# When GpSimd's indirect stores of rows may start: a table of waits in an attention and mixture-of-experts kernel

## The chip, the cores and the metric

The kernel runs on one core of a Trainium2 chip. The metric is the device time of one execution in microseconds (us). Three executions of the kernel before took 683.65 to 687.44 us, with a median of 686.25 us.

## What is computed

The reference runs a gated linear recurrence (an attention with a decaying state) and feeds its output to a mixture of experts. Cut to what matters:

```python
for t in range(S):                                   # attention, per batch and head
    S_re, S_im = (ar * S_re - ai * S_im + kv, ar * S_im + ai * S_re)   # kv = outer(k[t], v[t])
    y[:, :, t] = einsum('bhd,bhde->bhe', q[:, :, t], S_re)
x = y as [3072 tokens, 384]
noisy_logits = x @ w_gate + log1p(exp(x @ w_noise)) * noise            # 8 experts
top2 and their softmax weights
for e in range(8):                                   # each token goes to 2 of 8 experts
    out[mask] += top2_w * (relu(x[mask] @ w1[e]) @ w2[e])
```

## The kernel before, in words

The 3072 tokens are cut into 24 units of 128 tokens. Four units, one of each batch, make a group, so there are six groups; the code counts them 0 to 5, and the text calls them the first to the sixth group. An attention unit transposes its queries and keys on TensorE (`tr_unit`, L583) and copies them out on ScalarE (L584), forms scores (`sc_unit`, L593), masks them on VectorE (L594), and makes the output (`y_unit`, L642 and L644). `x_unit` (L652, L653) turns the output into rows of tokens in the tile `xr`.

When a group's rows are there, the gate picks two experts for each token (`gsel`, on ScalarE and VectorE), and `gdis` works out a slot for each choice: TensorE counts (L697, L699), and four VectorE instructions follow, L701 (positions), L703 (the running base), L704 and L707 (the slots, tile `sl`). Then `gscat` stores the rows: GpSimd issues one indirect store per unit and choice (L715), which sends 128 rows of 400 floats to the slots in the DRAM tensor `xs`. A group has eight such stores, and the kernel 48. The fifth and the sixth group are handled in two parts, of three units (`gscat4_0_3`, `gscat5_0_3`, six stores) and of one (`gscat4_3_4`, `gscat5_3_4`, two stores). The experts' phase loads rows from `xs` (L795, L797, L804). The first loads, of experts 0 and 1, wait only for the stores of the first three groups; the loads of the rest wait for all.

`xr` has three buffers. When a group opens a buffer again, GpSimd clears its last columns (MEMSET, L633) and copies the token numbers into it (L634). That MEMSET waits for the stores which read the buffer before, and it stands in GpSimd's queue between the stores.

Two tables set the order. `ORDER` lists, for TensorE (PE), ScalarE (ACT), VectorE (DVE) and SyncE (SP), every instruction of this phase in the sequence in which the engine runs them; `gdis3_0_4.0` is the first DVE instruction of `gdis` for group 3. GpSimd (POOL) has no list there. `PACE` adds waits: each entry makes one instruction wait for the end of a named instruction on another engine. Most entries concern the stores: `("POOL", "gscat3_0_4.2"): ("ACT", "gsel4_0_3.2")` lets the third store of group 3 start when that ScalarE instruction has ended. An engine works its queue in order, so what stands behind a waiting store on GpSimd waits too.

The loop that reads the table:

```python
for (e, t), (e2, t2) in PACE.items():
    tc.add_manual_dep(QUEUE[e, t][0], QUEUE[e2, t2][-1].name, later, reason="pace")
```

Of the kernel before, what the change touches and what calls it, by code (L numbers as in the profile page):

```python
# [187 lines left out]
        gsel3_0_4.6 gsel3_0_4.10 gsel3_0_4.7 gsel3_0_4.8 p319.0 st_upd16.0 gsel3_0_4.14 p3q19_0.0 sc_unit17_0.0  # L188
        sc_unit17_1.0 p322.0 st_scale15.0 gsel3_0_4.9 gsel3_0_4.12 gsel3_0_4.13 pick.4 gsel3_0_4.11 gsel3_0_4.16
        gsel3_0_4.17 p3q19_1.0 gsel3_0_4.15 gsel3_0_4.18 sc_unit18_0.0 gsel3_0_4.19 gsel3_0_4.22 gsel3_0_4.20  # L190
        st_upd17.0 sc_unit18_1.0 p321.0 p3q20_0.0 p3q21_0.0 p323.0 p3q20_1.0 gsel3_0_4.21 p3q22_0.0 st_upd18.0
        sc_unit19_0.0 sc_unit19_1.0 load_w10.0 gturn4_0_3.0 gsel4_0_3.0 p3q22_1.0 gdis3_0_4.0 gsel4_0_3.1 gsel4_0_3.2
        gdis3_0_4.1 x_G0_0.0 gsel4_0_3.3 load_w10.1 x_T0_0_0.0 gsel4_0_3.4 gsel4_0_3.5 gsel4_0_3.6 load_w10.2
        x_T0_0_1.0 gturn4_3_4.0 sc_unit20_0.0 gsel4_0_3.7 sc_unit20_1.0 gsel4_0_3.9 gsel4_3_4.0 x_T0_0_2.0 gsel4_0_3.8
        gsel4_3_4.1 gsel4_3_4.2 st_scale16.0 st_scale16.1 gdis3_0_4.2 gsel4_3_4.3 gsel4_0_3.11 gsel4_0_3.14 p3q21_1.0
        gsel4_0_3.15 x_G0_0.2 gsel4_0_3.12 p3q23_0.0 gsel4_0_3.10 mm10_0_1.0 gsel4_0_3.16 gsel4_0_3.17 gsel4_0_3.13
        gdis3_0_4.3 mm10_0_2.0 x_G0_0.1 mm10_0_1.1 gsel4_0_3.20 st_scale17.0 mm10_0_2.1 p3q23_1.0 gsel4_3_4.4
        st_upd19.1 st_upd23.0 gsel4_3_4.5 gsel4_3_4.6 st_upd15.0 sc_unit21_0.0 gsel4_0_3.18 sc_unit21_1.0 gsel4_3_4.7
        gdis4_0_3.0 gsel4_0_3.19 gdis4_0_3.1 load_w20_0_1_2.0 gsel4_3_4.10 gsel4_3_4.8 gsel4_3_4.9 st_scale19.0
        st_scale18.0 gsel4_3_4.16 gdis4_0_3.2 gdis4_0_3.3 load_w20_0_1_2.2 sc_unit22_0.0 gdis4_3_4.0 gdis4_3_4.1  # L200
# [72 lines left out]
}  # L273


# [1255 lines left out]
```

## Time and profile before

| | us |
|---|---|
| median of 3 executions | 686.25 |
| lowest and highest | 683.65, 687.44 |
| the profiled execution, its own time | 686.77 |
| span of its instructions in the trace | 685.1 |
| TensorE matmul busy in the span | 650.1 (95%) |
| VectorE busy | 435.1 (64%) |
| ScalarE busy | 367.9 (54%) |
| GpSimd busy | 174.9 (26%) |
| mean granted TensorE clock | 0.985 of full speed |

The busy shares are averages over unlike stages. Until about 268 us the kernel works on attention and gating, with expert 0's first matmuls between; from then on TensorE works through the experts. The chain that ended last is 77% TensorE and 11% VectorE.

### The profile page before, as it was taken

The page shows a single profiled execution, that of the slowest core. Times are in us where ns is not written, and L with a number is a line of the kernel's source. Part 1 is how long each engine was busy: PE and PEld are TensorE (multiplying, and loading weights), DVE is VectorE, ACT ScalarE, POOL GpSimd, SP SyncE. Part 2 cuts the span into 40 slices and gives each one's busy share as a digit, 9 for nine tenths or more (in the row PEclk, how much of TensorE's full clock was granted, in tenths as well). Part 3 has the DMA queues.
Part 4 walks back from the last instruction along what each step waited for, and adds up shares of the span by engine and source line. Part 5 has one row for each costly group of instructions (what it writes and reads, how often), then busy time and mean ns, then how long its engine had stood idle before and what let it go on. Part 6 is the DMA issues. An engine that isn't in the chain of part 4 may idle for free.

```text
span 685.1 us, 14285 instructions
## 1 busy us (share of the span) xinstructions
PE 650.1 (95%) x5505; PEld 573.5 (84%) x5505; DVE 435.1 (64%) x971; ACT 367.9 (54%) x610; POOL 174.9 (26%) x183
## 2 busy tenths in 40 slices
PE   8999999997989788999999999999999999999995
PEld 3468786876878577989899899899899899899895
DVE  7899999987778547546556526735735736746411
ACT  6999999987646345264423622732632732723300
POOL 3000000135230426002513302152142142163311
PEclk9999999999899889999999999999999999999998
DMA  6937766758386555278654756698598697682201
GB/s 240 295 113 205 212 158 211 199 177 258 118 249 182 184 165 171 87 252 236 173 159 118 264 143 203 198 192 223 189 166 250 193 186 228 194 219 91 83 36 35
DMA packets 120012, 124.24 MB, mean 181 GB/s; under 512 B 73610, under 2 KB 99104, under 8 KB 119936
## 3 DMA queue, kind: packets, MB, share of 16 engines
q1 hardware_dynamic: 110672, 95.76, 48.4%
q0 software_dynamic: 9264, 27.48, 13.3%
q8 instruction: 45, 0.74, 0.4%
q14 instruction: 31, 0.25, 0.1%
HBM read 70.11 MB, written 42.90 MB: 165 GB/s over the span
## 4 chain that ended last, share of the span: by engine, by line
PE 77%; DVE 11%; ACT 4%; another core or an unknown queue 2%; DMA 2%; issue 2%; SPq 1%; POOL 0%; POOLq 0%; ACTq 0%
PE ph L966 29%; PE po L1002 24%; PE po L1027 6%; PE ptr L583 3%; PE psc L593 2%; PE cum L533 2%; PE pY L642 2%; PE pY L644 1%; PE psc L966 1%; DVE qk L565 1%; DVE am L594 1%; DVE qh L573 1%; PE cum L652 1%; DVE im L528 1%
## 5 line engine op out<-in xcount | busy, mean ns | idle before, releaser
L966 PE MATMUL ph<-x,w1h 128*128 128x512 f32 (+4 forms) x720 | 184.7, 345 | 0.0
L1002 PE MATMUL po<-w2h,h 128*128 128x384 f32 x640 | 164.2, 335 | 0.0
L966 PEld LDWEIGHTS ph<-x,w1h 128*128 128x128 f32 x720 | 125.2, 188 | 14.9 <-DVE x L949 0.2
L987 POOL DMA_INDIRECT out_dram<-ao,ox x54 | 58.0, 1073 | 258.4 <-DVE ao L1015 155.4
L966 PE MATMUL ph<-x,w1l 128*128 128x512 f32 (+4 forms) x360 | 123.9, 344 | 0.0
L1002 PEld LDWEIGHTS po<-w2h,h 128*128 128x128 f32 x640 | 115.8, 188 | 0.3
L968 ACT ACTIVATE h<-ph 128x512 fp32r<-128x512 f32 (+4 forms) x120 | 60.7, 511 | 101.0 <-PE ph L966 82.2
L971 DVE SCALAR_TENSOR_TENSOR h<-ph,h 128x512 fp32r<-128x512 f32 (+5 forms) x128 | 69.3, 548 | 60.2 <-ACT h L968 55.3
L1002 PE MATMUL po<-w2l,h 128*128 128x384 f32 x320 | 107.0, 334 | 0.0
L715 POOL DMA_INDIRECT xs<-xr,sl x48 | 54.1, 1127 | 201.7 <-DVE kh L573 127.3
L1015 DVE SCALAR_TENSOR_TENSOR ao<-po,gw,ao 128x384 f32<-128x384 f32 (+1 forms) x42 | 25.7, 612 | 101.5 <-PE po L1002 101.3
L966 PEld LDWEIGHTS ph<-x,w1l 128*128 128x128 f32 x360 | 67.6, 188 | 7.6
L948 ACT CAST x<-xj 128x512 fp32r<-128x512 f32 (+4 forms) x39 | 20.7, 531 | 87.1 <-DVE xj L945 86.2
L978 POOL DMA_INDIRECT ao<-out_dram,ox x47 | 54.5, 1160 | 32.5 <-issue 28.8
L1002 PEld LDWEIGHTS po<-w2l,h 128*128 128x128 f32 x320 | 60.1, 188 | 0.2
L593 PEld LDWEIGHTS psc<-qT,kT 112*64 112x64 f32 x768 | 37.6, 143 | 5.9 <-issue 3.9
L593 PE MATMUL psc<-qT,kT 112*64 112x128 f32 (+1 forms) x768 | 41.1, 257 | 1.1 <-ACT kT L584 0.6
L644 PE MATMUL pY<-am,v 128*48 128x128 f32 x384 | 37.2, 277 | 5.0 <-issue 2.3
L594 DVE TENSOR_TENSOR am<-psc,mask 128x512 f32<-128x512 f32 x48 | 32.3, 680 | 13.6 <-PE psc L593 7.2
L1027 PE MATMUL po<-h,w2h 128*128 128x272 f32 (+2 forms) x192 | 38.7, 294 | 0.0
L949 DVE TENSOR_TENSOR x<-xj,x 128x512 fp32r<-128x512 f32 (+4 forms) x39 | 22.6, 579 | 24.1 <-ACT x L948 24.1
L584 ACT ACTIVATE kT<-ptr 112x1024 f32<-112x1024 f32 x24 | 24.8, 1032 | 22.7 <-remote 14.8
(246 smaller groups left out, 1113.4 us busy)
## 6 DMA issues: line engine op xcount, KB each, us to landing
raw<-in_moe_w_dram SPq DMA_DIRECT2D x24, 512.0 KB
raw<-in_moe_w_dram SPq DMA_DIRECT2D x32, 384.0 KB
qk<-in_qk_dram SPq DMA_DIRECT2D x24, 384.0 KB
v<-in_v_dram SPq DMA_DIRECT2D x24, 288.0 KB
xgb<-xs SPq DMA_DIRECT2D x8, 800.0 KB
xp<-xp SPq DMA_DIRECT2D x7, 768.0 KB
re<-in_a_dram SPq DMA_DIRECT2D x12, 384.0 KB
im<-in_a_dram SPq DMA_DIRECT2D x12, 384.0 KB
```

Of the source, the lines that this page charges most:

```text
L593: nc.tensor.matmul(p[o:o + 64, j, z:], KT[n][:, h, z:z + 64], QT[n][:, h, z:], start=True, stop=True, skip_group_check=True)
L594: nc.vector.tensor_mul(AM[n][:, 4 * half:4 * half + 4, :].rearrange("p (a r) t -> p a (r t)", r=2), p.rearrange("p (a r) t -> p a (r t)", ...
L644: nc.tensor.matmul(o, V[n][:, H + h // 2 if h % 2 else h, :], AM[n][:, h, :], start=not g, stop=True, skip_group_check=True)
L715: d = nc.gpsimd.indirect_dma_start(out=xs, out_offset=bass.IndirectOffsetOnAxis(ap=sl[:, kk, b:b + 1], axis=0), in_=XR[g][:, lo + b, :], i ...
L966: nc.tensor.matmul(p[:, :n], W1[e, kk][i][:, f * 128:(f + 1) * 128], XW[w, kk][:, j, :], start=(c == 0), stop=(c == len(ms) - 1))
L968: highs.append(nc.scalar.activation(h[:, 0:n], p[:, :n], AF.Relu))
L971: d = nc.vector.scalar_tensor_tensor(h[:, dst:dst + b - a], p[:, a:b], 0.0, h[:, a:b].bitcast(F32), op0=OP.max, op1=OP.subtract)
L978: nc.gpsimd.indirect_dma_start(out=ao[j][0:w, :], out_offset=None, in_=out, in_offset=bass.IndirectOffsetOnAxis(ap=OX[e][0:w, j:j + 1], ax ...
L987: d = nc.gpsimd.indirect_dma_start(out=out, out_offset=bass.IndirectOffsetOnAxis(ap=OX[e][0:n, j:j + 1], axis=0), in_=a, in_offset=None, b ...
L1002: nc.tensor.matmul(p[:, :DM], HT[w, f][i][:, o:o + 128], W2[f // 2][k2][:, f % 2, :], start=(m == 0), stop=(m == len(ms) - 1))
L1015: kept.append(nc.vector.scalar_tensor_tensor(a, p[0:n, :DM], g, a, op0=OP.mult, op1=OP.add))
L1027: nc.tensor.matmul(p[:, :n], W2[f // 2][k2][:, f % 2, kk * 128:(kk + 1) * 128], HT[0, f][i][:, 0:n], start=(m == 0), stop=(m == len(ms) - 1))
```

## The change

Only the two tables change; every instruction stays, with the same operands. In `PACE` the entries of the stores are replaced. Before, stores of a group were tied to ScalarE instructions many of which end before the group's slots are known, and the entries of a group did not follow the order of its stores. Now the stores go in their order 0, 1, 2, ..., the first of a group waits only for the slots (in the sixth group's first part for a ScalarE instruction too), and each later one waits for an instruction of its own, of ScalarE or, in four cases, of VectorE. In `ORDER` the four VectorE instructions `gdis3_0_4.0` to `.3` move up. A cut of the diff:

```diff
 ORDER["DVE"]:
-        st_upd17.0 sc_unit18_1.0 p321.0 p3q20_0.0 p3q21_0.0 p323.0 p3q20_1.0 gsel3_0_4.21 p3q22_0.0 st_upd18.0
-        sc_unit19_0.0 sc_unit19_1.0 load_w10.0 gturn4_0_3.0 gsel4_0_3.0 p3q22_1.0 gdis3_0_4.0 gsel4_0_3.1 gsel4_0_3.2
-        gdis3_0_4.1 ...
+        st_upd17.0 sc_unit18_1.0 p321.0 p3q20_0.0 p3q21_0.0 p323.0 p3q20_1.0 gsel3_0_4.21 gdis3_0_4.0 gdis3_0_4.1
+        gdis3_0_4.2 gdis3_0_4.3 p3q22_0.0 st_upd18.0 ...
 PACE, second group:
-    ("POOL", "gscat1_0_4.0"): ("ACT", "gsel2_0_4.0"), ("POOL", "gscat1_0_4.6"): ("ACT", "p317.1"), ...
+    ("POOL", "gscat1_0_4.1"): ("ACT", "p319.1"), ("POOL", "gscat1_0_4.2"): ("ACT", "x_unit9.0"),
+    ("POOL", "gscat1_0_4.3"): ("ACT", "y_unit13.0"), ("POOL", "gscat1_0_4.4"): ("ACT", "x_unit11.0"),
+    ("POOL", "gscat1_0_4.5"): ("ACT", "p2s10.0"), ("POOL", "gscat1_0_4.6"): ("ACT", "y_unit14.0"),
+    ("POOL", "gscat1_0_4.7"): ("ACT", "p2t22.0"),
 PACE, third group:
+    ("POOL", "gscat2_0_4.1"): ("ACT", "tr_unit17_0.0"), ("POOL", "gscat2_0_4.2"): ("ACT", "p2s11.1"),
+    ("POOL", "gscat2_0_4.3"): ("ACT", "p320.1"), ("POOL", "gscat2_0_4.4"): ("ACT", "gsel3_0_4.0"), ...
 PACE, fourth and fifth group:
-    ("POOL", "gscat3_0_4.0"): ("ACT", "load_w10.0"), ("POOL", "gscat3_0_4.5"): ("ACT", "glog4_0_3.0"),
-    ("POOL", "gscat3_0_4.3"): ("ACT", "gsel4_0_3.1"), ("POOL", "gscat3_0_4.7"): ("ACT", "x_T0_0_1.0"),
-    ("POOL", "gscat3_0_4.2"): ("ACT", "gsel4_0_3.2"), ("POOL", "gscat3_0_4.6"): ("ACT", "x_unit18.0"),
+    ("POOL", "gscat3_0_4.1"): ("ACT", "load_w10.0"),
+    ("POOL", "gscat3_0_4.2"): ("ACT", "gsel4_0_3.0"), ("POOL", "gscat3_0_4.3"): ("ACT", "gsel4_0_3.1"),
+    ("POOL", "gscat3_0_4.4"): ("ACT", "glog4_3_4.0"), ("POOL", "gscat3_0_4.5"): ("ACT", "gsel4_3_4.0"),
+    ("POOL", "gscat3_0_4.6"): ("DVE", "p3q21_1.0"), ("POOL", "gscat3_0_4.7"): ("DVE", "gsel4_0_3.10"),
+    ("POOL", "gscat4_0_3.1"): ("ACT", "gsel4_3_4.2"), ("POOL", "gscat4_0_3.2"): ("ACT", "load_w20_0_1_2.1"), ...
```

On VectorE, at the end of the fourth group's gate choice, the difference is this; `xr<-ga4t` (L318) is the last instruction of `gsel3_0_4`, `pos` and `sl` belong to the fourth group, and `kh` and `qh` are attention's:

```order
 L573 TENSOR_TENSOR kh_123<-qk,tr 128x2x8x48
 L318 TENSOR_TENSOR xr<-ga4t 128x4x8
+L701 TENSOR_TENSOR pos_2895<-cum,base_run 128x32
+L703 TENSOR_TENSOR base_run<-base_run,cum 128x8
+L704 TENSOR_TENSOR ga4oh<-ga4oh,pos_2895 128x64
+L707 TENSOR_REDUCE sl_2899<-ga4oh 128x8
 L573 TENSOR_TENSOR qh_121<-qk,tr 128x2x8x48
 L614 TENSOR_TENSOR z_646<-z_646,pG 112x384
```

The four stood 8, 10, 31 and 44 rows further down; nothing else on VectorE changes place.

On GpSimd, the stores of the fourth group (`sl_2899`) and of the fifth group's first part (`sl_3339`) stood before as follows, with what each waits for in brackets (DMASW are completions of earlier indirect transfers):

```order
L715 DMA xs<-xr,sl_2899 24576x400 [waits DVE_49,Activation_49,Pool_49]
L715 DMA xs<-xr,sl_2899 24576x400
L715 DMA xs<-xr,sl_2899 24576x400 [waits Activation_49]
L715 DMA xs<-xr,sl_2899 24576x400 x5
L715 DMA xs<-xr,sl_3339 24576x400 [waits DVE_49,DMASW0_49,Activation_49,Pool_49]
L715 DMA xs<-xr,sl_3339 24576x400 [waits DMASW1_49]
L715 DMA xs<-xr,sl_3339 24576x400 [waits DMASW2_49]
```

and stand now so:

```order
L715 DMA xs<-xr,sl_2899 24576x400 [waits DVE_49,Pool_49]
L715 DMA xs<-xr,sl_2899 24576x400 [waits Activation_49] x5
L715 DMA xs<-xr,sl_2899 24576x400 [waits DVE_49] x2
L715 DMA xs<-xr,sl_3339 24576x400 [waits DMASW0_49,DVE_49,Pool_49]
L715 DMA xs<-xr,sl_3339 24576x400 [waits DMASW1_49,Activation_49]
L715 DMA xs<-xr,sl_3339 24576x400 [waits DMASW2_49,Activation_49]
```

Seven of the eight stores now have a wait of their own; before, five followed one another without one. Two smaller moves on GpSimd: the clearing of the `xr` buffer for the fourth group stands behind two stores of the second group instead of four, and the last of the sixth group's stores comes after the two of its second part.

## Rows read from the trace of the kernel before

**Rows 1.** The page, part 1: busy time of each engine in the span.

```profile
PE 650.1 (95%) x5505; PEld 573.5 (84%) x5505; DVE 435.1 (64%) x971; ACT 367.9 (54%) x610; POOL 174.9 (26%) x183
```

**Rows 2.** Busy time by stretch; the first line names the columns.

```profile
core 0: us, PE busy (x) PEld busy (x) DVE busy (x) ACT busy (x) POOL busy (x), PEclk, DMA share, GB/s
...
160.00:165.00 5.00, 4.70 (x91) 3.65 (x92) 4.96 (x10) 4.75 (x8) 4.22 (x6) 1.00 0.92 249
...
195.00:200.00 5.00, 5.00 (x106) 4.77 (x103) 4.36 (x21) 1.82 (x4) 2.35 (x2) 1.00 0.87 228
205.00:222.00 17.00, 17.00 (x235) 15.36 (x232) 14.55 (x46) 11.32 (x24) 0.99 (x2) 1.00 0.62 183
...
228.00:236.00 8.00, 3.92 (x31) 1.85 (x29) 4.45 (x17) 0.00 (x0) 5.40 (x6) 0.89 0.59 203
236.00:242.00 6.00, 5.12 (x48) 4.30 (x49) 1.41 (x2) 3.36 (x5) 1.94 (x2) 0.58 0.88 295
242.00:247.00 5.00, 2.94 (x40) 2.41 (x38) 1.23 (x5) 0.29 (x1) 2.92 (x3) 1.00 0.53 206
...
268.00:680.00 412.00, 409.24 (x2376) 384.79 (x2376) 215.54 (x426) 162.44 (x276) 119.11 (x107) 1.00 0.62 174
```

**Rows 3.** The chain that ended last, 215 to 270 us: start, duration, what.

```profile
227.72 8.76 another core or an unknown queue
...
240.74 5.89 another core or an unknown queue
```

**Rows 4.** VectorE's waits, 120 to 290 us: us in total, times, longest.

```profile
DVE pos L701 <- remote: 7.0, 2, 4.1
...
DVE tf L539 <- ACT tf L538: 2.5, 1, 2.5
DVE am L594 <- PE cum L533: 2.3, 1, 2.3
```

**Rows 5.** Timeline of GpSimd: start, duration, instruction, idle time before it and its releaser.

```profile
133.15 1.75 POOL L715 DMA_INDIRECT xs<-xr,sl  x1 [127.33 <-DVE kh L573]
...
178.11 0.97 POOL L715 DMA_INDIRECT xs<-xr,sl  x1 [9.84 <-ACT tr L468]
...
185.10 0.99 POOL L715 DMA_INDIRECT xs<-xr,sl  x1 [0.61 <-POOL xr L634]
...
224.83 1.16 POOL L715 DMA_INDIRECT xs<-xr,sl  x1 [18.23 <-DVE ohs L688]
...
233.95 0.97 POOL L715 DMA_INDIRECT xs<-xr,sl  x1 [0.30 <-issue]
239.52 0.97 POOL L715 DMA_INDIRECT xs<-xr,sl  x1 [4.59 <-DVE w2l L870]
...
244.62 0.97 POOL L715 DMA_INDIRECT xs<-xr,sl  x1 [0.30 <-issue]
```

**Rows 6.** Timeline of VectorE, 130 to 224 us.

```profile
132.05 1.82 DVE L573 TENSOR_TENSOR kh<-qk,tr 128x768 f32<-128x768 f32 x2
...
193.98 1.32 DVE L594 TENSOR_TENSOR am<-psc,mask 128x512 f32<-128x512 f32 x2 [2.76 <-PE psc L593]
...
204.52 0.95 DVE L573 TENSOR_TENSOR kh<-qk,tr 128x768 f32<-128x768 f32 x1
205.39 0.18 DVE L318 TENSOR_TENSOR xr<-ga4t 128x32 f32<-128x32 f32 x1
...
222.83 0.16 DVE L304 FIND_INDEX8 ga3ix<-ga3mx,ga3c 128x8 uint32<-128x8 f32 x1
...
223.80 0.22 DVE L707 TENSOR_REDUCE sl<-ga4oh 128x8 uint32<-128x64 f32 x1
```

**Rows 7.** Timeline of ScalarE: three of the instructions that stores now wait for.

```profile
156.25 0.47 ACT L468 ACTIVATE ee<-cum 128x384 f32<-128x384 f32 x1
...
175.96 1.05 ACT L538 ACTIVATE tf<-cum,small 128x384 f32<-128x384 f32 x2
...
206.94 1.06 ACT L870 CAST w1h<-raw 128x1024 fp32r<-128x1024 f32 x1
```

More of the change, by code (lines that the diff above doesn't have):

```diff
@@ L190 @@
         gsel3_0_4.17 p3q19_1.0 gsel3_0_4.15 gsel3_0_4.18 sc_unit18_0.0 gsel3_0_4.19 gsel3_0_4.22 gsel3_0_4.20
-        st_upd17.0 sc_unit18_1.0 p321.0 p3q20_0.0 p3q21_0.0 p323.0 p3q20_1.0 gsel3_0_4.21 p3q22_0.0 st_upd18.0
-        sc_unit19_0.0 sc_unit19_1.0 load_w10.0 gturn4_0_3.0 gsel4_0_3.0 p3q22_1.0 gdis3_0_4.0 gsel4_0_3.1 gsel4_0_3.2
[L193 to L197, printed above, removed]
+        st_upd17.0 sc_unit18_1.0 p321.0 p3q20_0.0 p3q21_0.0 p323.0 p3q20_1.0 gsel3_0_4.21 gdis3_0_4.0 gdis3_0_4.1
+        gdis3_0_4.2 gdis3_0_4.3 p3q22_0.0 st_upd18.0 sc_unit19_0.0 sc_unit19_1.0 load_w10.0 gturn4_0_3.0 gsel4_0_3.0
+        p3q22_1.0 gsel4_0_3.1 gsel4_0_3.2 x_G0_0.0 gsel4_0_3.3 load_w10.1 x_T0_0_0.0 gsel4_0_3.4 gsel4_0_3.5
+        gsel4_0_3.6 load_w10.2 x_T0_0_1.0 gturn4_3_4.0 sc_unit20_0.0 gsel4_0_3.7 sc_unit20_1.0 gsel4_0_3.9 gsel4_3_4.0
+        x_T0_0_2.0 gsel4_0_3.8 gsel4_3_4.1 gsel4_3_4.2 st_scale16.0 st_scale16.1 gsel4_3_4.3 gsel4_0_3.11 gsel4_0_3.14
+        p3q21_1.0 gsel4_0_3.15 x_G0_0.2 gsel4_0_3.12 p3q23_0.0 gsel4_0_3.10 mm10_0_1.0 gsel4_0_3.16 gsel4_0_3.17
+        gsel4_0_3.13 mm10_0_2.0 x_G0_0.1 mm10_0_1.1 gsel4_0_3.20 st_scale17.0 mm10_0_2.1 p3q23_1.0 gsel4_3_4.4
         st_upd19.1 st_upd23.0 gsel4_3_4.5 gsel4_3_4.6 st_upd15.0 sc_unit21_0.0 gsel4_0_3.18 sc_unit21_1.0 gsel4_3_4.7
```

33 rows, old and new, of the table PACE are left out of this document.

## The prediction

> **What bounds the kernel now.** I read the page first: TensorE's matmuls are busy for 650.1 of 685.1 us [rows 1], so it looks like a kernel with nothing to gain outside TensorE. That is an average, so I read busy time by stretch next. From 268 us to 680 us TensorE is busy for 409.24 of 412 us [rows 2]: this stage is bound by its matmuls, no store into `xs` stands in most of it, and the change doesn't touch it. Whatever the change gives or takes must come ahead of 268 us, and is then carried to the end one for one. Ahead of 268 us there are holes. From 228 to 236 us TensorE issues 31 matmuls and is busy for 3.92 of 8 us, where a normal stretch of attention, 195 to 200 us, has 106 in 5 us; ScalarE does nothing in these 8 us [rows 2]. The chain that ended last has two pieces in this region that it can put to no engine, 8.76 us at 227.72 and 5.89 us at 240.74 [rows 3]. VectorE has two waits of the same kind, 7.0 us together, the longer 4.1 us [rows 4]; both are for counts that TensorE had already issued. So in these holes TensorE has taken in its work and doesn't finish it.
>
> What goes on beside them is read from GpSimd's timeline. Between the stores that start at 224.83 and at 233.95 us lie six others, one each 1.27 to 1.46 us; between 239.52 and 244.62 us lie three, at the same pitch [rows 5]. The two holes of the chain begin some 3 and 1 us after the first store of each row. Against this, the store at 178.11 us stands alone, 10 us after its forerunner [rows 5], and nothing of that sort follows it. I take it from this that **stores in a row stall TensorE, and a store by itself doesn't**. Why is not in the trace: in 228 to 236 us the DMA share is 0.59, while TensorE runs undisturbed at 0.87 in 195 to 200 us [rows 2], so full DMA engines alone don't explain it.
>
> **The change part by part.** Nothing is added or removed but waits, so every term is a hole that goes, stays or comes. I work on the profiled execution, 686.77 us.
>
> Fourth group. Its slots come from L707 at 223.80 us, though the gate's last instruction, L318, ends near 205.6 us [rows 6]; the four VectorE instructions that follow now stand right behind it. TensorE's list has the counts that they read (`gdis3_0_4.0`) ahead of the transposes of unit 20, so VectorE should find them done; the four take 0.8 us (four at 0.18 to 0.22 [rows 6]), which VectorE saves further down, and I cost the move at nothing. If VectorE had to wait there, `qh` and `z` behind it would start late by that wait. GpSimd then has eight stores with slots at about 206.5 us instead of 224.0. They wait for instructions that run from 206.94 us (`load_w10.0`, L870) to 222.83 us (`gsel4_0_3.10`, L304) [rows 6, 7], seven of them, so the pitch is some 2.5 us instead of 1.3. Behind a waiting store on GpSimd stands only the next store; the next clearing of `xr` is ahead of this group. The hole at 227.72 us loses its stores: 8.76 us [rows 3], of which I leave 0.8 for the transposes that ScalarE's copy must await anyway, so **8.0 us**. From 236 to 242 us the granted clock is 0.58 [rows 2], that is mostly the lower level, 1.2 GHz, after the idle stretch; 5.12 us busy at 0.58 are 3.0 at full speed: **2.1 us** more, of which I take 2.
>
> Fifth group, first part. The first store follows the slots, the next four wait for a ScalarE instruction each, so the five in a row part. The hole is 5.89 us in the chain [rows 3], 2.06 us of idle TensorE [rows 2], and 2.9 us (7.0 less 4.1) in VectorE's wait [rows 4]. I take **3 us**, VectorE's figure, since it is the one of one wait; the others are the ends.
>
> Second group. VectorE is full in 160 to 165 us, 4.96 of 5 [rows 2], so here its waits count: 4.1 us for the counts [rows 4], and 2.5 us for `tf` [rows 4], which comes after the clock has fallen. Its stores now wait for seven instructions between 156.25 and 175.96 us [rows 7], 2.8 us apart on average. At most 6.6 us go; this part of the kernel also has the DMA engines full, 0.92 [rows 2], and loads on which VectorE may wait next, so I take **4 us**.
>
> First group. VectorE waits 2.3 us behind its first stores [rows 4]. The first two still follow each other closely. I take **1 us** of 0 to 2.3.
>
> Third group. Its stores start when the clearing of the `xr` buffer is done, which waits for the second group's last store (in before, that of 178.11 lets the row begin at 185.10 us [rows 5]). The instructions named stand early in this stretch (unit 17's transposes, the next group's `p320`, the first steps of the gate), so most of these stores find their wait already over and go in a row. Before, the row began at 185.10 us, and VectorE lost 2.76 us [rows 6]. Now the price may be that of the fourth group's row, 8.76 us for eight, 1.1 us each: 6.0 us more than before. The later names still hold the last stores back if the engines slow down. I take a **loss of 2 us** between 0 and 6.
>
> Spaced stores where there were none. In 205 to 222 us TensorE is busy for 17.00 us of 17 and VectorE for 14.55 [rows 2]; a hole there would be on the path. Eight stores come in. The lone store says 0 each, the row says 1.1 each: 0 to 8.8 us. The DMA share there is 0.62; the share of 228 to 236 us, stores for the most part, is 0.59 of 8 us [rows 2], so the row adds about 4.7 us of full DMA engines to 10.5 us in 17, and still fits. I am nearest to the lone store and take a **loss of 1 us**.
>
> Sum: 8 + 2 + 3 + 4 + 1 - 2 - 1 = 15 us, and 686.8 - 15 = 671.8 us. The profiled execution stands 0.5 us over the median of the runs, so I say **671.5 us**. What is late next where the holes go: TensorE's own matmuls in 205 to 260 us, then the serial chain of the last gate before 268 us, which the change leaves alone.
>
> **The rivals.** (a) *All holes go, and the third group's row costs no more than before*: 8.8 + 2.1 + 5.9 + 6.6 + 2.3 = 25.7, so 661 us. Against it: the two figures of the fifth group differ, and something is always next.
>
> (b) *A store costs TensorE the same wherever it stands in attention.* Then the holes only move: the fourth group's 8.8 us to 206 to 223 us, the others stay. That is 686 us, no change. For it: every hole has stores beside it, and the first group's first stores already cost VectorE 2.3 us [rows 4, 5]. Against it: the lone store.
>
> (c) *Slower: price per store, and a denser row.* As (b), but the third group's eight, now at 1.3 us, cost 8.8 us instead of 2.8: 686.8 + 6 = 693 us. It decides from the point where a spaced store costs more than about 0.9 us, since fourteen of them, eight of the fourth group and six of the fifth, then give back the 13 us counted for these groups.
>
> (d) *VectorE pays.* Stores take longer when VectorE works on two inputs: 1.75 us at 133.15, against 0.97 us [rows 5]. If VectorE lost the excess, 0.78 us, at each of the eight stores in 205 to 222 us, 6.2 us would be lost there: 678 us. Two `kh` products, of which the second runs under the store of 133.15 us, take 1.82 us, and one without a store 0.95 us [rows 6]; so it is the store that stretches, and VectorE doesn't slow. The Trainium skill bears on this (GPSIMD Engine Reference, section Specifications): GpSimd shares its SBUF interfaces with VectorE and contends with VectorE instructions that have two SBUF inputs. By that rule the move of eight stores under a busy VectorE speaks against this change, to the sum just given; the trace shows the contention on the store's side alone.
>
> (e) *The waits don't space.* Where the holes go, the named instructions move together, and those of the fifth group come as quickly as the stores. Then its 3 us stay: 675 us, within the forecast.
>
> **How the numbers follow.** Forecast with (e), 665 to 680 us: 0.69. (a), below 665: 0.08. (d), 675 to 681: 0.05. (b) and mixtures of it, 683 to 689: 0.11. (c), above 689: 0.07. The range of 662 to 683 us leaves out (b), (c) and the end of (a). A measurement of this kernel can tell about 0.5%, 3.4 us, from no change. Faster by more than that, under 682.8: 0.82; within it: 0.11; slower: 0.07.
>
> **What would show it.** In the profile of the changed kernel GpSimd's timeline should have the fourth group's stores some 2 to 3 us apart, about 15 us ahead of their old place, and the chain no unassigned pieces of 8.76 and 5.89 us. Matmul counts by stretch should stay near 20 per us through the fourth and fifth groups. The third group's row should show a hole with fewer than 10 matmuls per us. Expert 0's L1002 should begin near 253 us instead of 268, and the stretch after it should last as long as before, with TensorE as full. I am wrong if matmuls thin out beside spaced stores too (then b or c), or if VectorE's own instructions grow longer beside them (d).

## The result, and the profile after

The changed kernel takes **668.95 us**, median of 6 executions (668.53 to 671.38), against 685.99 us of the kernel before in 6 executions on the same chip (683.65 to 688.15). The ratio is 0.9744, with a 95% interval of 0.9722 to 0.9766: 17 us less. The profiled execution took 669.0 us with a span of 667.2 us; before it was 686.77 and 685.1. The forecast was 671.5 us, with a range of 662 to 683.

Busy time by stretch, after (columns as in [rows 2]). The stretches from 125 to 250 us and from 250 us on are what lies ahead of expert 0's first layer and behind it; the others are places that the prediction speaks of:

```profile
125.00:250.00 125.00, 119.16 (x1747) 101.61 (x1745) 104.12 (x327) 88.51 (x155) 51.15 (x49) 0.99 0.69 212
...
165.00:170.00 5.00, 4.55 (x69) 3.54 (x69) 4.70 (x11) 3.32 (x5) 3.13 (x3) 1.00 0.79 261
...
180.00:185.00 5.00, 4.46 (x22) 3.20 (x22) 1.24 (x3) 1.07 (x4) 2.33 (x4) 0.67 0.33 126
...
205.00:222.00 17.00, 16.24 (x212) 14.62 (x213) 14.01 (x50) 9.95 (x22) 6.03 (x6) 1.00 0.64 218
...
228.00:236.00 8.00, 7.69 (x135) 6.68 (x132) 4.92 (x10) 5.34 (x9) 3.82 (x4) 1.00 0.74 247
...
250.00:667.00 417.00, 409.20 (x2376) 384.78 (x2376) 215.97 (x425) 162.02 (x275) 119.85 (x108) 1.00 0.61 172
```

And the stretch of before that holds the same work as the first of these lines:

```profile
125.00:268.00 143.00, 125.25 (x1747) 105.66 (x1745) 104.20 (x329) 89.21 (x155) 50.68 (x50) 0.94 0.60 186
```

The same 1747 matmuls took 143 us and take 125. Of the 18 us, TensorE was idle for 11.9 (143.00 - 125.25 = 17.75 before, 125.00 - 119.16 = 5.84 after) and busy for 6.1 us longer, at a granted clock of 0.94 instead of 0.99. Behind it nothing changed: 2376 matmuls in 409.20 us, where [rows 2] have 2376 in 409.24. From 228 to 236 us, where there were 31 matmuls and no work on ScalarE, there are 135.

GpSimd's timeline, after: the third to fifth of the third group's stores, the fourth group's first four, and the fifth group's first four.

```profile
178.99 1.31 POOL L715 DMA_INDIRECT xs<-xr,sl  x1 [0.30 <-issue]
180.60 0.98 POOL L715 DMA_INDIRECT xs<-xr,sl  x1 [0.30 <-issue]
181.89 0.97 POOL L715 DMA_INDIRECT xs<-xr,sl  x1 [0.30 <-issue]
...
202.45 0.99 POOL L715 DMA_INDIRECT xs<-xr,sl  x1 [9.79 <-DVE sl L707]
203.75 0.97 POOL L715 DMA_INDIRECT xs<-xr,sl  x1 [0.30 <-issue]
207.06 1.18 POOL L715 DMA_INDIRECT xs<-xr,sl  x1 [2.33 <-ACT ga3w L468]
209.73 0.97 POOL L715 DMA_INDIRECT xs<-xr,sl  x1 [1.49 <-ACT ga3w L468]
...
228.73 0.97 POOL L715 DMA_INDIRECT xs<-xr,sl  x1 [7.71 <-issue]
230.00 0.97 POOL L715 DMA_INDIRECT xs<-xr,sl  x1 [0.30 <-issue]
233.73 1.56 POOL L715 DMA_INDIRECT xs<-xr,sl  x1 [2.76 <-ACT w2h L870]
235.68 1.67 POOL L715 DMA_INDIRECT xs<-xr,sl  x1 [0.39 <-ACT lt L664]
```

The fourth group's stores now start at 202.45 us, 22 us ahead of the row in [rows 5] (some 18 of it because the slots were moved up, the rest because the work ahead of them ends sooner), and from the third on they stand some 2.7 us apart, the last 2.3. The third group's first five go in a row, and in 180 to 185 us stand 22 matmuls, at a clock of 0.67. The chain that ended last has no piece of "another core or an unknown queue" between 125 and 265 us any more; VectorE's wait for the counts, 7.0 us in two [rows 4], is down to these:

```profile
DVE pos L701 <- PE ptr L583: 1.5, 1, 1.5
DVE pos L701 <- PE cum L697: 1.2, 1, 1.2
```

Expert 0's first layer, the point from which nothing differs, begins in the chain at

```profile
250.21 8.45 PE po L1002 x48
```

and began at 268.34 us before: 18.1 us sooner. This one time serves below to read each experiment's profile.

### The profile page after: what moved, and what is told of

Same layout as the page of the kernel before. It is cut to its first block, busy times and chain, and to the rows that moved or that the text cites. A ratio compares the mean times of both kernels' runs of the same rounds, so it can differ in the third digit from the quotient of the medians.

```text
span 667.2 us, 14284 instructions
## 1 busy us (share of the span) xinstructions
PE 643.3 (96%) x5502; PEld 569.3 (85%) x5505; DVE 435.8 (65%) x971; ACT 366.9 (55%) x610; POOL 176.2 (26%) x183
## 4 chain that ended last, share of the span: by engine, by line
PE 83%; DVE 8%; ACT 4%; issue 2%; DMA 1%; SPq 1%; POOL 0%; POOLq 0%; ACTq 0%; DVEq 0%
PE ph L966 30%; PE po L1002 25%; PE po L1027 6%; PE ptr L583 4%; PE psc L593 3%; PE pY L642 2%; PE pY L644 2%; PE cum L533 2%; PE psc L966 2%; PE cum L560 1%; PE pG L605 1%; PE cum L652 1%; DVE qk L565 1%; DVE am L594 1%; PE cum L661 1%
## 5 line engine op out<-in xcount | busy, mean ns | idle before, releaser
L715 POOL DMA_INDIRECT xs<-xr,sl x48 | 57.4, 1195 | 186.7 <-DVE kh L573 128.8
L593 PEld LDWEIGHTS psc<-qT,kT 112*64 112x64 f32 x768 | 35.6, 137 | 5.1 <-issue 3.7
L593 PE MATMUL psc<-qT,kT 112*64 112x128 f32 (+1 forms) x768 | 39.2, 250 | 0.5 <-issue 0.5
L642 PE MATMUL pY<-qT,z 112*48 112x128 f32 x320 | 32.5, 276 | 1.2 <-issue 1.2
```

The source lines that it names most:

```text
L593: nc.tensor.matmul(p[o:o + 64, j, z:], KT[n][:, h, z:z + 64], QT[n][:, h, z:], start=True, stop=True, skip_group_check=True)
L642: nc.tensor.matmul(o, Z[b][:, h, :], QT[n][:, h, :], start=True, stop=False, skip_group_check=True)
L715: d = nc.gpsimd.indirect_dma_start(out=xs, out_offset=bass.IndirectOffsetOnAxis(ap=sl[:, kk, b:b + 1], axis=0), in_=XR[g][:, lo + b, :], i ...
```

## The experiments

Each kernel was compared with the kernel before on the chip on which it ran; that one's median was 685 to 688 us there, so differences of medians between runs of different chips are good to some 2 us only, and the ratio is the safer figure.

| kernel | median us | ratio to before (95%) | expert 0 begins, us |
|---|---|---|---|
| before | 685.99 | 1 | 268.34 |
| after | 668.95 | 0.9744 (0.9722 to 0.9766) | 250.21 |
| third group spaced too | 664.63 | 0.9693 (0.9652 to 0.9733) | 245.40 |
| fourth group in a row | 674.43 | 0.9831 (0.9795 to 0.9867) | 256.37 |
| spacing alone | 677.42 | 0.9872 (0.9835 to 0.9908) | 262.37 |
| slots sooner alone | 686.39 | 0.9992 (0.9955 to 1.0029) | 268.49 |
| all groups in rows, slots sooner | 694.97 | 1.0118 (1.0079 to 1.0156) | 272.74 |
| third spaced, 5 extra stores | 667.72 | 0.9738 (0.9704 to 0.9771) | 251.39 |
| the same, a third of the bytes | 668.17 | 0.9757 (0.9720 to 0.9793) | 250.01 |
| the same, a quarter of the rows | 668.99 | 0.9757 (0.9725 to 0.9789) | 251.59 |
| the same, plain transfers | 664.65 | 0.9700 (0.9665 to 0.9734) | 246.46 |
| third spaced, two pairs parted | 662.87 | 0.9639 (0.9613 to 0.9665) | 244.70 |

My theory was that indirect stores issued one right behind the other stall TensorE and that stores some 2 us apart don't. The main rival was rival (b), a price per store wherever it stands; others were that the slots sooner, or the place, carry the gain.

**Third group spaced too.** On the changed kernel:

```diff
-    ("POOL", "gscat2_0_4.1"): ("ACT", "tr_unit17_0.0"), ("POOL", "gscat2_0_4.2"): ("ACT", "p2s11.1"),
-    ("POOL", "gscat2_0_4.3"): ("ACT", "p320.1"), ("POOL", "gscat2_0_4.4"): ("ACT", "gsel3_0_4.0"),
-    ("POOL", "gscat2_0_4.5"): ("ACT", "gsel3_0_4.1"), ("POOL", "gscat2_0_4.6"): ("ACT", "p321.1"),
-    ("POOL", "gscat2_0_4.7"): ("ACT", "p322.0"),
+    ("POOL", "gscat2_0_4.1"): ("ACT", "tr_unit17_1.0"), ("POOL", "gscat2_0_4.2"): ("ACT", "y_unit16.0"),
+    ("POOL", "gscat2_0_4.3"): ("ACT", "p322.0"), ("POOL", "gscat2_0_4.4"): ("ACT", "tr_unit18_1.0"),
+    ("POOL", "gscat2_0_4.5"): ("DVE", "p322.0"), ("POOL", "gscat2_0_4.6"): ("ACT", "y_unit17.0"),
+    ("POOL", "gscat2_0_4.7"): ("ACT", "tr_unit19_0.0"),
```

> The changed kernel, with the third group's last seven stores waiting for operations some 2 us apart as the other groups' do, in place of going in a row. If stores in a row hold TensorE up and spaced ones do not: the stretch from 180 to 185 us, which has 22 matmuls now where its neighbours have 51 to 106, fills up, expert 0's first layer starts 2 to 5 us sooner, and the whole kernel takes 664 to 667 us against 669. If each store has its price wherever it stands: 669. If the stretch is thin for another reason (an operation of ScalarE or VectorE that ends late): 669, and the stretch stays thin without the row.

Measured: 664.63 us, and expert 0 begins at 245.40 us, 4.8 us sooner. The stretch that was thin, in this kernel:

```profile
180.00:185.00 5.00, 5.00 (x53) 3.80 (x53) 4.42 (x13) 4.94 (x11) 3.43 (x3) 1.00 0.55 164
```

53 matmuls instead of 22, the clock at 1.00, VectorE busy for 4.42 us instead of 1.24. The hole was the row's. A price per store falls here: the kernel has the same 48 stores.

**Fourth group in a row, at its new place.** On the changed kernel, the seven waits are taken out:

```diff
-    ("POOL", "gscat3_0_4.1"): ("ACT", "load_w10.0"), ("POOL", "gscat3_0_4.2"): ("ACT", "gsel4_0_3.0"),
-    ("POOL", "gscat3_0_4.3"): ("ACT", "gsel4_0_3.1"), ("POOL", "gscat3_0_4.4"): ("ACT", "glog4_3_4.0"),
-    ("POOL", "gscat3_0_4.5"): ("ACT", "gsel4_3_4.0"), ("POOL", "gscat3_0_4.6"): ("DVE", "p3q21_1.0"),
-    ("POOL", "gscat3_0_4.7"): ("DVE", "gsel4_0_3.10"),
```

> The changed kernel, without the seven waits of the fourth group's stores: they go in a row at the same place, from some 202 us on, with the same slots. If rows are what costs: a hole between 203 and 214 us and 5 to 9 us more, 674 to 678 us against 669. If each store has its price wherever it stands, or if it was only the place of the old row (224 to 236 us) that was bad: 669 to 670.

Measured: 674.43 us, 5.5 us more than the changed kernel, and expert 0 6.2 us later. The row starts at 203.59 us; the timeline of three engines and one stretch show what it does:

```profile
203.59 0.99 POOL L715 DMA_INDIRECT xs<-xr,sl  x1 [10.39 <-DVE sl L707]
203.89 1.07 PE L661 MATMUL cum<-xT,wg 128*32 128x128 f32 x24
204.88 0.97 POOL L715 DMA_INDIRECT xs<-xr,sl  x1 [0.30 <-issue]
204.90 1.08 PE L583 MATMUL ptr<-ident,kh 128*112 128x128 f32 x8
206.16 1.32 POOL L715 DMA_INDIRECT xs<-xr,sl  x1 [0.31 <-issue]
...
208.74 0.26 ACT L664 COPY lt<-cum 96x128 f32<-96x128 f32 x1 [4.27 <-remote]
...
205.50:209.00 3.50, 0.48 (x5) 0.23 (x3) 1.14 (x2) 0.26 (x1) 2.65 (x3) 1.00 0.53 146
```

By the trace, the 24 matmuls of L661 end at 204.96 us. ScalarE's copy of their result, with nothing ahead of it in its queue since 204.47 us, starts at 208.74, 3.8 us later. The same copy in the kernel before, with no store in the 8 us ahead of it, started 0.06 us behind the matmuls' end:

```profile
208.54 0.26 ACT L664 COPY lt<-cum 96x128 f32<-96x128 f32 x1 [0.55 <-PE cum L661]
```

In the changed kernel, behind the pair of 202.45 and 203.75 us, it starts 1.6 us behind their end (205.44 us). Meanwhile TensorE has run the next transposes and then, waiting for ScalarE in turn, stands still, as all the others but GpSimd do. This is how the row costs here: the matmuls were issued in time, and what waits for them goes on late. The Trainium skill (Perfetto Trace Analysis, section Tensor Engine Instruction) says that the trace's end of a matmul is computed, and that the completion is sent only once PSUM has acknowledged the write. By that the result may really have been late, or only its message; this row fits both, and no run here tells them apart.

**Spacing alone.** The changed kernel with `gdis3_0_4.0` to `.3` at their old places on VectorE; all new waits stay:

```diff
-        gsel3_0_4.21 gdis3_0_4.0 gdis3_0_4.1 gdis3_0_4.2 gdis3_0_4.3 p3q22_0.0 ...
+        gsel3_0_4.21 p3q22_0.0 ... p3q22_1.0 gdis3_0_4.0 gsel4_0_3.1 gsel4_0_3.2 gdis3_0_4.1 ...
```

> The changed kernel, with the fourth group's four slot operations back at their old places on VectorE, so that this group's slots are ready after the operations that its stores wait for, and they go in a row. If rows are what costs: the fourth group's hole of some 9 us is back, 676 to 681 us against 669, and the first, second and fifth group's gains stay. If the slots sooner carry all: 686. If spacing alone carries all: 669.

Measured: 677.42 us, 8.5 more than the changed kernel. The fourth group's slots come when the instructions that its stores wait for are over, the eight go in a row from 224.7 us on, and the chain has its piece back:

```profile
227.56 8.81 another core or an unknown queue
```

That is [rows 3] again, 8.76 us. The profiled execution is the longest of four (680.2 us), and shows by accident one more case. GpSimd's timeline in the second group, and the stretch after it:

```profile
159.88 0.12 POOL L633 MEMSET xr<- 128x28 f32 x1 [0.92 <-DMA xd<-xr]
...
161.04 0.99 POOL L715 DMA_INDIRECT xs<-xr,sl  x1 [0.40 <-ACT kT L584]
162.34 1.74 POOL L715 DMA_INDIRECT xs<-xr,sl  x1 [0.30 <-issue]
164.39 0.97 POOL L715 DMA_INDIRECT xs<-xr,sl  x1 [0.31 <-issue]
165.66 0.98 POOL L715 DMA_INDIRECT xs<-xr,sl  x1 [0.30 <-issue]
...
165.00:170.00 5.00, 2.17 (x4) 1.26 (x5) 3.47 (x10) 1.80 (x3) 2.26 (x3) 0.71 0.84 267
```

A transfer that came late held up the clearing of `xr`, the stores behind it moved together, four went 1.3 to 2.1 us apart, and 4 matmuls stand where the changed kernel has 69. The waits themselves were the same. I read it so that a wait on another engine's work makes a distance only as long as GpSimd isn't late; this is one execution, and no run tests it.

**Slots sooner alone.** The kernel before, with the four VectorE instructions moved as in the change, and with before's waits:

```diff
-        gsel3_0_4.21 p3q22_0.0 ... p3q22_1.0 gdis3_0_4.0 gsel4_0_3.1 gsel4_0_3.2 gdis3_0_4.1 ...
+        gsel3_0_4.21 gdis3_0_4.0 gdis3_0_4.1 gdis3_0_4.2 gdis3_0_4.3 p3q22_0.0 ...
```

> The kernel before, with nothing but the fourth group's four slot operations moved up on VectorE; the waits of the stores stay as before, so the fourth group's stores can start near 206 us and then follow the old waits, which are spread over ScalarE's operations there. If a row of stores is what costs: the hole of 8.76 us goes as far as the old waits space the stores, 676 to 682 us against 686; where they leave them in a row, the hole only moves and the time stays at 685 to 687. If the whole gain came from the slots being ready sooner: 669 to 671. If each store has its price: 686.

Measured: 686.39 us, no change. The stores start at 210.3 us, and the first three go in a row (210.3, 211.6, 212.8 us); the chain of this kernel has

```profile
210.90 3.95 another core or an unknown queue
```

and the hole of 8.76 us at 227.72 is gone. Against the profile of before, block by block as in the table further down: up to 200 us this execution is already 2.9 us behind, in groups that the edit doesn't touch; it loses 3.3 us in 205 to 231 us, where the smaller row stands; it wins 9.1 at the old row's place; and it loses 3.0 in the fifth and the sixth group, which still go in rows. That is 0.1 us behind at expert 0. So a part of the null is this execution's chance, but the 10 executions' median agrees with it: without the new waits the move is worth 3 us at most (the lower end of the interval, 0.9955, is 3.1 us off 686). I had expected 676 to 682 us where the old waits space the stores, and this was a miss: from the fourth store on they do space them (215.4, 219.2, 221.3, 228.0 us, with only the last at 229.3 us close behind), and yet the median gains nothing. The row of three takes back a third of what the old row's place gives; where the rest goes, other than the chance of one execution, stays open.

**All groups in rows.** The changed kernel without any of the waits of the stores; slots as in the change:

```diff
-    ("POOL", "gscat0_0_4.1"): ("ACT", "y_unit11.0"), ("POOL", "gscat0_0_4.2"): ("ACT", "glog2_0_4.0"),
...
-    ("POOL", "gscat5_0_3.4"): ("ACT", "load_w11.1"), ("POOL", "gscat5_0_3.5"): ("DVE", "x_T1_0_0.0"),
```

> The changed kernel without any of the waits of GpSimd's stores: all six groups' stores go as soon as their slots are there, so in rows; the fourth group's slots stay early. If rows are what costs, the sum of the groups' prices: 5 to 6 us for the fourth (as its row alone cost), 5 to 7 for the second, 2 to 3 for the first, 4 to 6 for the fifth, against 669: 684 to 691 us. If the price goes by the number of stores: 669.

Measured: 694.97 us, 1.2% slower than the kernel before, and 26 us more than the changed kernel. That is beyond what I had expected of the sum, and what the excess is was not looked into. The third group shows a row's effect best:

```profile
190.00:195.00 5.00, 0.26 (x1) 0.26 (x2) 2.86 (x11) 1.50 (x5) 2.54 (x5) 0.67 0.34 130
```

One matmul starts in 5 us, beside and behind the last of eight stores from 182.14 to 191.89 us. The DMA share is 0.34, so here the DMA engines are far from full. This is the whole value of the waits: the same instructions on the same data, 26 us apart.

The same profile shows where a row does no harm. Six stores of the sixth group go 1.27 to 1.29 us apart from 268.24 to 274.63 us, and from 272.60 us on, where expert 0's first layer runs, TensorE has no gap:

```profile
272.60:276.00 3.40, 3.40 (x22) 3.40 (x23) 2.95 (x12) 3.00 (x5) 2.68 (x3) 1.00 0.39 149
```

So the stall is shown for attention and gating alone. No run tells what makes the difference.

**What of a row costs: bytes, rows, or stores.** To the kernel with the third group spaced, five stores are added behind that group's last; they wait, as that last store does, for `tr_unit19_0.0`, and write a constant tile into a scratch table:

```diff
+        for i in range(5 if g == 2 else 0):
+            d = nc.gpsimd.indirect_dma_start(
+                out=xn, out_offset=bass.IndirectOffsetOnAxis(ap=sl[:, i % 2, i // 2:i // 2 + 1], axis=0),
+                in_=none[:, :], in_offset=None, bounds_check=E * N - 1, oob_is_err=False)
...
```

The second has `none[:, 0:128]` and a table of 128 floats a row, the third `sl[0:32, ...]` and `none[0:32, :]`, the fourth `nc.gpsimd.dma_start(out=xn[128 * i:128 * i + 128], in_=none)`.

> The kernel with the third group spaced, and right behind that group's last store five extra indirect stores in a row (128 rows of 400 floats each, from a constant tile into a scratch table that nobody reads, by the third group's slots), in 192 to 199 us, where 16 to 32 matmuls start in a us. Nothing of the computation is left out. If stores in a row hold TensorE up, whatever they carry and whoever needs them: a hole there and 4 to 8 us more, 668 to 673 us against 664.6. If it was the wait of the tokens' own data or slots that cost, not the stores: 665.

> As the kernel with five extra stores, but each of their rows has 128 floats in place of 400, so 0.32 of the bytes and the same rows and instructions. If the bytes that they move hold TensorE up: a third of the extra stores' price, 666 to 668 us. If it is the number of rows (a descriptor each) or of store instructions: as much as the full ones, 668 to 673.

> As the kernel with five extra stores, but of 32 rows of 400 floats each in place of 128, so a quarter of the rows and of the bytes and as many instructions. If the price goes by rows or by bytes: a quarter of the extra stores' price, 665.5 to 667 us. If it goes by store instructions in a row: as much as the full ones, 668 to 673.

> As the kernel with five extra stores, but plain transfers from GpSimd's queue, each of the same 128 rows of 400 floats from the constant tile to consecutive rows of the scratch table, with no slots. If the price is that of the rows' addresses being worked out on GpSimd, 664 to 666 us; if it is that of the bytes or of the writing to DRAM, as the full indirect ones, 668 to 673.

All four ran on one chip. The plain ones cost nothing that the medians can tell (664.65 us; expert 0 begins 1.1 us later than without them); the indirect ones cost 3.1, 3.5 and 4.3 us more than the plain ones, which can't be told apart with four executions each. At expert 0's start they are 4.9, 3.6 and 5.1 us later than with plain transfers. GpSimd's timeline for the full stores, then for those of 32 rows, and then for the plain ones:

```profile
191.32 0.97 POOL L719 DMA_INDIRECT xs<-xr,sl  x1 [0.45 <-ACT qT L588]
192.60 4.92 POOL L729 DMA_INDIRECT xn<-none,sl  x1 [0.30 <-issue]
197.82 1.31 POOL L729 DMA_INDIRECT xn<-none,sl  x1 [0.30 <-DMA raw<-in_moe_w_dram]
199.43 0.97 POOL L729 DMA_INDIRECT xn<-none,sl  x1 [0.30 <-issue]
```

```profile
192.61 0.89 POOL L729 DMA_INDIRECT xn<-none,sl  x1 [0.30 <-issue]
193.80 1.43 POOL L729 DMA_INDIRECT xn<-none,sl  x1 [0.30 <-issue]
195.54 1.43 POOL L729 DMA_INDIRECT xn<-none,sl  x1 [0.30 <-issue]
```

```profile
191.56 2.77 POOL L729 DMA_DIRECT2D xn<-none  x5
```

And the stretch with the hole, for the full stores and for those of 32 rows:

```profile
200.00:205.00 5.00, 1.21 (x10) 0.79 (x10) 1.07 (x1) 0.26 (x1) 3.92 (x7) 0.77 1.02 288
```

```profile
195.00:200.00 5.00, 3.52 (x33) 2.29 (x31) 2.29 (x4) 1.02 (x1) 3.66 (x6) 0.77 0.71 228
```

Ten and 33 matmuls, where the kernel without extra stores has 94 and 80. A quarter of the rows and of the bytes, or a third of the bytes, stalls TensorE about as much as the whole. So the price comes with indirect stores issued behind one another and hardly depends on what they move, and nobody needs to wait for their data: nothing reads the scratch table. All three have five extra stores, so how the price goes with their number isn't shown. One limit: the first full extra store itself stood 4.92 us on GpSimd, so the row proper began only at 197.82 us and ran on into the fourth group's stores; the variants don't stall at the same spot, and their prices compare only roughly.

**Two pairs parted.** On the kernel with the third group spaced, the second store of the fourth and of the fifth group waits for a later instruction:

```diff
-    ("POOL", "gscat3_0_4.1"): ("ACT", "load_w10.0"),
+    ("POOL", "gscat3_0_4.1"): ("DVE", "load_w10.0"),
...
-    ("POOL", "gscat4_0_3.1"): ("ACT", "gsel4_3_4.2"),
+    ("POOL", "gscat4_0_3.1"): ("DVE", "gdis4_3_4.1"),
```

> The kernel with the third group spaced, and the second store of the fourth and of the fifth group, each 1.3 us behind the first there, moved to a wait some 2 us later. If two stores at that distance already cost something: 0.5 to 1.5 us less than the kernel with the third group spaced, 663 to 664 us. If a pair is free: 664.6, as that one.

Measured: 662.87 us (5 executions, 661.92 to 663.31). Its ratio, 0.9639, has an interval that still overlaps with that of the kernel with pairs, and expert 0 begins 0.7 us sooner: a pair may cost something, less than these runs can settle. In the fourth group the pair only moved by one store, as GpSimd's timeline shows:

```profile
198.32 0.99 POOL L715 DMA_INDIRECT xs<-xr,sl  x1 [0.70 <-POOL xr L634]
201.49 0.97 POOL L715 DMA_INDIRECT xs<-xr,sl  x1 [2.18 <-DVE lz L671]
202.76 0.98 POOL L715 DMA_INDIRECT xs<-xr,sl  x1 [0.30 <-issue]
```

It is the fastest kernel here, 24.5 us or 3.6% below the kernel before on its chip (687.34 us).

## Why the prediction was right

**The bound and the carry.** I said that from 268 us on the kernel is bound by its matmuls and that a gain ahead of it is carried one for one. It is: 18.1 us at expert 0, 17.9 in the span.

**The terms.** TensorE runs the same order before and after, so the same matmuls can be compared in both traces. The start of a block of L605 or of the counts (L699), before and after, gives the gain up to there, and the difference from one to the next is the term:

| between | start of the block at its end, before, after | gain so far | term | predicted |
|---|---|---|---|---|
| ahead of the first group's stores | 131.9, 131.6 | 0.3 | 0.3 | 0 |
| first group | 144.0, 141.9 | 2.1 | +1.8 | +1 |
| second group | 176.4, 169.0 | 7.4 | +5.3 | +4 |
| third group | 200.8, 196.2 | 4.6 | -2.8 | -2 |
| spaced stores, 205 to 222 us | 224.9, 221.6 | 3.3 | -1.3 | -1 |
| fourth group's old place | 241.7, 229.3 | 12.4 | +9.1 | +10 |
| fifth group | 259.9, 243.3 | 16.6 | +4.2 | +3 |
| sixth group, to expert 0 | 268.1, 250.0 | 18.1 | +1.5 | not in the sum |

Every term has the sign and about the size that I gave it; the sum was 15 us and came to 18. What was missing is the sixth group, whose stores the sum left out though the change spaces them too (I had said that the last gate is left alone), and about 1 us each in the first, the second and the fifth group. That single terms agree to 1 us is in part luck. The kernel with the slots sooner alone has the first three groups as before, and yet its execution differs from that of before in them, by -2.5, +2.1 and -3.1 us (plus is sooner); what is firm is the whole, 18 us here and 17 by the medians. For the fifth group I took VectorE's 2.9 us between 2.06 and 5.89; it came to 4.2, between VectorE's figure and the chain's 5.89. The clock is a part of the gain that I counted only at one place, 2 us; over the whole stretch TensorE is busy for 6.1 us less on the same matmuls.

**Loss in the third group.** Said and found: the row, the thin stretch, the low clock. What I couldn't tell from the trace of before is that this is a cost without any need: spaced, the group gives back 4.3 us by the medians, 3.5 by the ratios (0.0051 of 686).

**Spaced stores.** I priced them near the lone store, 1 us for all, between 0 and 8.8. It is 1.3, and the only hole in 205 to 222 us (16.24 us of 17 busy) stands behind the pair of 202.45 and 203.75 us, where ScalarE's copy of L664 came 1.6 us late. Experiments with the same number of stores lie 32 us apart (662.87 and 694.97), so rival (b), a price per store, falls, and with it (c).

**The move of the slots** I put together with the spacing and gave them 10 us for the fourth group. Alone, spacing lacks 8.5 us of the whole, since waits can space nothing when the slots come after the instructions that they name; and the slots sooner alone bring nothing that can be measured. So the 10 us belong to the two together. That VectorE would find the counts done was right: behind L318, L701 starts without a wait at 200.83 us in the trace.

**Rival (d), VectorE pays.** VectorE's groups and GpSimd's stores, before and then after (line, instruction, count | busy, mean ns of one | idle before):

```profile
L573 DVE TENSOR_TENSOR kh<-qk,tr 128x768 f32<-128x768 f32 x24 | 22.6, 948 | 0.0
```

```profile
L573 DVE TENSOR_TENSOR kh<-qk,tr 128x768 f32<-128x768 f32 x24 | 22.6, 951 | 1.1 <-remote 1.0
```

Before, a store took 1127 ns in the mean (54.1 us for 48), now it takes 1195 (57.4 us for 48); VectorE's product went from 948 to 951 ns. So VectorE doesn't pay; GpSimd's stores take 3.3 us more in all, off the path. Whether this is the contention that the Trainium skill describes (GPSIMD Engine Reference, section Specifications) no run here tests. In the trace of the changed kernel all 19 stores longer than 1.05 us run beside VectorE instructions with two inputs, but so do ten of the 29 short ones, for 0.9 us and more; the prediction's sentence that stores take longer then is not a rule.

**Rival (e)** came in part: three of the fifth group's first part stand 1.8 to 2.0 us apart (235.68, 237.66 and 239.49 us in the trace) instead of 2 to 3. It didn't cost the 3 us.

## What to carry to other kernels

When the trace shows a hole in which every engine but one waits, and the chain can put it to nobody, look at the rhythm of the engine that still works, not at how much it moves: here, in attention and gating, rows of GpSimd's indirect stores 1.3 us apart stop the other engines for some 4 to 9 us, and stores 2 to 3 us apart cost next to nothing. Small waits on other engines' work are enough to give such stores a rhythm, but they only do so while their data are ready before the work that they wait for; so the data have to be early, and the two edits belong together (spacing without the early slots lacked 8.5 us). Give every group the waits: the one left in a row here was worth a fifth to a quarter of the whole gain.

## What the runs showed of the hardware that I had not expected

- The stall comes with indirect stores in a row and hardly goes by their rows or bytes: five extra of 128 rows of 1600 bytes cost 3.1 us, of 128 rows of 512 bytes 3.5, of 32 rows of 1600 bytes 4.3, each against five plain transfers of the same queue, which cost nothing that can be told (0.9700 against 0.9693).
- In the stall TensorE's work is issued and by the trace done, but the engine that waits for it goes on late, by 3.8 us in the case shown and again with all groups in rows (218.19 us), 1.6 us behind a pair of stores and 0.06 us with no store near. Why is open. The granted clock is low in it or behind it (0.58 to 0.77 in [rows 2] and the stretches above), so a stall costs twice.
- Six indirect stores in a row beside expert 0's first layer left no gap in TensorE's work (3.40 us busy of 3.40).
- An indirect store of 128 rows right behind the third group's last stood 4.92 us on GpSimd (4.90 with rows of 512 bytes), where its forerunner took 0.97; one of 32 rows took 0.89. No run looked into it.
